# One shifted copy of VectorE's key tiles made by GpSimd in 128x512 pieces, and key products released three slots later

## The chip, the core and the metric

The kernel runs on one core of a Trainium2 chip. The metric is device time in microseconds, from the first to the last instruction and what lies around them; the median of the runs is compared. Engines are called as in the profile: PE (TensorE, matrix products), ACT (ScalarE, exponentials), DVE (VectorE), POOL (GpSimd) and SP (SyncE, whose queue issues most transfers).

## What is computed

A gated mix of an attention block with 32 heads of width 16 and a feed-forward block, for one sequence of 2048 rows of width 512:

```python
qkv = (x @ wqkv).reshape(B, S, 3, H, Dh).transpose(2, 0, 3, 1, 4)
q, k, v = qkv[0], qkv[1], qkv[2]
scores = einsum("bhqd,bhkd->bhqk", q, k) * (Dh ** -0.5)
a = einsum("bhqk,bhkd->bhqd", softmax(scores), v).transpose(0, 2, 1, 3).reshape(B, S, D) @ wo
b = (silu(x @ w_gate) * (x @ w_up)) @ w_down
g = sigmoid((x * gate_w).sum(-1, keepdims=True))
out = g * a + (1 - g) * b
```

The softmax needs 32 x 2048 x 2048 exponentials, far more than anything else that the vector engines do.

## The kernel before

**Units and key tiles.** The 2048 queries are cut into 4 blocks of 512, the 32 heads into 8 groups of 4. A pair of a query block and a head group is a unit; there are 32, and the four units of head group 0 come first. Each unit has 16 key tiles of 128 keys; a key tile is 4 heads x 128 keys x 512 queries, so there are 512 key tiles. A key tile's position in the whole run is a slot.

**Two ways to an exponential.** For most key tiles PE writes scores into a two-bank PSUM tile `s_t`, and ACT makes the exponentials of both banks in one instruction into `e_all` (128x1024). The rest go to DVE. PE writes their scores, head by head, into one-bank tiles `d_t` (function `emit_d`), often beside an `s_t` group in other rows of the array. DVE reads each `d_t` out of PSUM, scales it and adds a constant, and writes it as 16-bit integers: read as bf16, that bit pattern is a first approximation of the exponential (`first`, one instruction of 128x512 for each head, four into one tile `y` of 128x2048). The approximation is then refined in one of two ways. With `groups[n] == 4` DVE makes three copies of `y`, each shifted by another constant (`copy`, one 128x2048 integer addition each, `SHIFTS`), and PE sums `y` and the three copies against the values: four sums over the key tile. With `groups[n] == 2` DVE makes two masked copies (`bits`) and multiplies (`product`, a 128x2048 product of two tensors): two sums. `quad` chooses the second way unless the planner has found idle room on PE.

**Buffers.** `y` and its copies live in seven homes of 128x2048 (`NS`, `home`, `take_home`, `drop`): six of their own (`c_t` in the profile), and as the seventh a piece of memory that belongs to `wd_t` early and to `kaug` later; so the same operation appears in the profile with `c_t`, `wd_t` or `kaug` in its name. A home is free again when PE has summed the copy, or, for `y`, also when DVE no longer reads it.

**What sets the order.** Every instruction of PE, ACT, DVE and SP is put in a fixed order by hand (`ordered`): each follows the one recorded before it on its engine. A planner in the program keeps an estimated time for each engine (`plan.pe`, `plan.dve`, `plan.act`), and picks what to record next. `fill_dve` picks DVE's next work: evictions of `d_t` (`d_wait`, `pay_d`), other evictions that are owed (`owed`, `pay`), and copies, masks and products (`vops`, `pay_v`). The prices are constants in the program. `v_unit` decides whether another key tile goes to DVE, from how far DVE lags behind ACT in the plan.

**Side work on PE.** Query, key and value products, the feed-forward block and the output projection are chains of pieces with a first slot and a deadline (`Pacer`, `pace.add(pieces, release, deadline, ...)`), put between the score groups. `k_pieces(b, tb)` makes the keys of two head groups for one block of 512 rows (`kp` from `xT` and `wqk`); its result goes through `kst` (the tiles `on` or `bblk`) and is sent by DMA from SP into `kaug`, the key tile with four heads at rows 0, 32, 64 and 96. `k0_pieces(tb)` makes the keys of head group 0 directly (`kp` from `xT` and `mt`, where a padded copy of the weights lies).

**Start of the program.** SP loads the rows and transposes of x (`xT`), then the rest of the value weights (`rb`), then the rest of `wqk`. ACT's queue loads the first columns of the weights. The first two score groups need only those.

In the profile, line 168 is the helper that records every PE product, line 171 the one of ACT, line 180 the one of DVE and SP. POOL has memsets of the start alone (lines 254 to 282, 521, 522).

Of the kernel before, what the change touches and what calls it, by code (L numbers as in the profile page):

```python
# [9 lines left out]
ALU = mybir.AluOpType  # L10
# [69 lines left out]
def kernel(  # L80
# [12 lines left out]
    nc = tc.nc  # L93
# [79 lines left out]
    class Ordered:  # L173
# [4 lines left out]
        def __getattr__(self, name):  # L178
            f = getattr(self.engine, name)
            return lambda *a, **kw: ordered(f(*a, **kw))  # L180

    vec = Ordered(nc.vector)
    queue = Ordered(nc.sync)


# [105 lines left out]


    class Plan:
        pe = dve = act = 0.0
        mode = last = None
        seq = 0
        slot = -1
# [13 lines left out]
    FLIP, UNIT_US = 0.105, 0.217  # L311
    TO_ACT, ACT_FIX, ACT_COL, ACT_IN = 0.485, 0.064, 0.4265, 0.167
    ACT_PE, DVE_PE, PE_DVE, ACT_DVE = 0.055, 0.08, 0.24, 0.06

    def spend(mode, mms, ready=0.0):

# [5 lines left out]
    def later(cost, f, ready=None, key=None):  # L322

        c = plan.chain
        if c is not None:
            c.owed += 1
        ready = plan.pe + PE_DVE if ready is None else ready
        owed.insert(sum(o[0] <= ready for o in owed), (ready, cost, f, c, key))

    def spend_v(cost, ready=0.0, key=None):  # L330

        if key is not None and key == plan.last:
            cost += 0.13
        plan.last = key
        plan.dve = max(plan.dve, ready) + cost
# [115 lines left out]
    def k_pieces(b, tb):  # L451

        def end(t, p):
            vec.tensor_copy(out=kst[b][:, t * QBW:(t + 1) * QBW], in_=p[:, :])
            m_free(p, plan.dve)
            if t == QB - 1:
                for hh in range(8):
                    g, j = 2 * b + hh // 4, hh % 4
                    if g > 0:
                        queue.dma_start(out=kaug[32 * j:32 * j + DH, g, :], in_=kst[b][DH * hh:DH * (hh + 1), :])  # L460

        def lhs(dc):
            if dc == 0 and tb == 0:
                kst[b] = (on_t[1], bblk)[b == 1][:, :, :].rearrange("p b q -> p (b q)")
            return wqk[:, dc, D + P * b:D + P * (b + 1)]
        return columns(DC, "kp", lhs, lambda dc: xT[:, dc, tb * QBW:(tb + 1) * QBW],
                       lambda p: later(0.6, lambda: end(tb, p)))
# [365 lines left out]
        users[i] = [1, 0.0]  # L833
        return i, t

    def home(i=None, t=0.0):

        if i is None:
            i, t = take_home()
        plan.dve = max(plan.dve, t)  # L840
        if i < NS - 1:
            return i, vex.tile([P, NV * QBW], U16, tag=f"h{i}", name="c_t", bufs=1)[:, :]
        return i, (kaug[:, 0, :] if au > QB else wd_t[:, 0:4, :].rearrange("p f d -> p (f d)")).bitcast(U16)

    def emit_d(i, rows=32):
        if not vcur:
            n = v_take()
            waiting[n] = [NV, None, take_home()]
            vcur.update(n=n, left=list(range(NV)), y=None)
            y_live[0] += 1  # L850
        n, left, cur = vcur["n"], vcur["left"], waiting[vcur["n"]]
        left.remove(i)
        d_t = m_tile("d_t")
        score(d_t[:, :], 4 * n + i, rows)
        if not left:
            vcur.clear()

        def first():
            if cur[1] is None:
                cur[1] = home(*cur[2])  # L860
            h, y = cur[1]
            vec.tensor_scalar(out=y[:, i * QBW:(i + 1) * QBW], in0=d_t[:, :], scalar1=EXP_A, scalar2=EXP_B[groups[n]],
                              op0=ALU.mult, op1=ALU.add)
            m_free(d_t, plan.dve)
            cur[0] -= 1
            if cur[0]:
                return
            plan.last = ("y", n)
            if groups[n] == 2:
                vops.extend([(0.6, lambda: bits(n, 0, y), ("y", n), n, True), (0.6, lambda: bits(n, 1, y), None, n, True),  # L870
                             (MUL_US, lambda: product(n, h, y), None, n, False)])
            else:
                users[h][0] = 2
                ready(n, 0, h, y)
                for k in range(1, 4):
                    vops.append((0.6, lambda k=k: copy(n, k, h, y), ("y", n) if k == 1 else None, n, True))
        d_wait.append((plan.pe + UNIT_US + PE_DVE, first, n))

    waiting = {}
# [4 lines left out]
        copies[n, k] = (c.bitcast(BF16), h)  # L884
        vready.append((plan.dve + DVE_PE, n, k))

    def copy(n, k, i, y):
        h, c = home()
        vec.tensor_scalar(out=c, in0=y, scalar1=SHIFTS[k - 1], scalar2=None, op0=ALU.add)
        ready(n, k, h, c)  # L890
        if k == 3:
            drop(i, plan.dve + 0.05)
            y_live[0] -= 1

# [16 lines left out]
    def c_ready():  # L911
        return min(c_free) if not vops or vops[0][4] else 0.0
# [5 lines left out]

    def pay_v():
        cost, f, key, _, _ = vops.pop(0)  # L920
        spend_v(cost, 0.0, key)
        f()

    def fill_dve():

        while plan.dve <= plan.pe + 0.2:
            now = plan.dve
            due = [k for k, o in enumerate(owed) if o[0] <= now + 0.05]
            free = [k for k in due if owed[k][4] is None or owed[k][4] != plan.last]
            fit = bool(vops) and vops[0][3] // KT <= closed + AHEAD and c_ready() <= now  # L930
            if fit and vops[0][3] // KT < au and vops[0][2] != plan.last:
                pay_v()
            elif d_wait and d_wait[0][2] // KT < au and d_wait[0][0] <= now + 0.05:
                pay_d()
            elif free:
                pay(free[0])
            elif d_wait and d_wait[0][0] <= now + 0.05:
                pay_d()
            elif fit and vops[0][2] != plan.last:
                pay_v()  # L940
            elif due:
                pay(due[0])
            elif fit:
                pay_v()
            elif d_wait or owed or vops and vops[0][3] // KT <= closed + AHEAD:
                t = min([w[0] for w in d_wait] + [o[0] for o in owed[:1]]
                        + [c_ready()] * bool(vops and vops[0][3] // KT <= closed + AHEAD))
                if t > plan.pe:
                    break
                plan.dve = max(plan.dve, t)  # L950
                plan.last = None
            else:
                break
# [330 lines left out]
    for qb in range(QB):  # L1284
        for b in range(NB):
            d = UNIT.index((qb, max(2 * b, 1))) * KT
            after = []
            if qb == 0:
                ks = []
                for tb in range(QB):  # L1290
                    prev = [pace.add(k_pieces(b, tb), 0, d - 40 + tb, prev)]
                    ks += prev

                def bnd(b=b):
                    later(2.46, lambda: k_bound(b))
                after = prev = [pace.add([(0.2, bnd, False)], 0, d - 34, ks)]

            if b == 0:
                rel = UNIT.index((qb - 1, 2)) * KT + 1 if qb else 0
            elif b == 1:  # L1300
                rel = UNIT.index((qb - 1, 6)) * KT + 1 if qb else 0
            else:
                rel = UNIT.index((qb, 2 * b - 2)) * KT + 1 if (qb, b) != (0, 2) else UNIT.index((0, 2)) * KT + 1
            q = pace.add(q_pieces(qb, b), rel, d - QLEAD, after)
            need.setdefault(d - 12, []).append(q)
            for g in {max(2 * b, 1), 2 * b + 1}:
                q_of[UNIT.index((qb, g))] = q
# [182 lines left out]
    def next_pv():  # L1490
        flush_act()
        while not pv_list(None):
            if d_wait:
                pay_d()
            elif vops and c_ready() < 1e9:
                pay_v()
            elif owed:
                pay()
            else:
                lone_d()  # L1500
        emit_pv(pv_list(None)[0])
# [105 lines left out]
                continue  # L1607
        emit_group(w, ride, rel)
    flush_act()
    while closed < UNITS or vops or vcur:  # L1610
        fill_dve()
        while owed and owed[0][0] <= plan.pe:
            pay()
        if plan.slot < SLOTS + 1:
            begin(plan.slot + 1)
            pace.credit = max(pace.credit, 2.0)
        if vcur:
            lone_d()
            continue
        c = side(2.0)  # L1620
        if not pv_list(plan.pe) and c is not None:
            put_piece(c)
            continue
        if closed == UNITS - 1 and pv_left(closed) <= 2 and not a_ps[2:]:
            tail_ready()
            tail(3)
        next_pv()
# [72 lines left out]
```

## Time and profile before

| | us |
|---|---|
| three runs | 773.22, 774.35, 776.6 |
| median | 774.35 |
| profiled execution, time | 773.97 |
| profiled execution, span from first to last instruction | 772.3 |
| PE busy | 743.8 (96%) |
| DVE busy | 737.9 (96%) |
| ACT busy | 751.0 (97%) |
| POOL busy | 10.6 (1%) |
| granted clock, mean | 0.996 |

The span is shorter than the time by 1.7 us, which lie around the first and the last instruction. A busy time is the union of an engine's instructions; consecutive instructions of DVE and ACT overlap a little, so the mean duration of one is longer than the step from one start to the next. A row of a group gives the instructions' line, engine, operation and tiles, how many there are, then their busy time in microseconds and the mean of one in nanoseconds, then the idle time in front of them and what ended it. A row of a wait gives who waited for whom, the sum in microseconds, how often, and the longest.

### The profile page before, as it was taken

What the parts mean: (1) busy time and instruction counts of PE and PEld (TensorE: products, weight loads), DVE (VectorE), ACT (ScalarE), POOL (GpSimd) and SP (SyncE); (2) the same over time, 40 slices, a digit from 0 to 9 for tenths busy, and PEclk for the clock granted to TensorE, in tenths of its full rate; (3) what the DMA queues carried; (4) which work ended last, traced back from release to release, by engine and by line L of the source; (5) the groups of instructions that cost most, each with busy time, mean ns of one, the idle gap of its engine ahead of it and who ended that gap; (6) DMA issues with size and microseconds to landing.
All of it is one profiled execution on the core that took longest, in us unless ns stands there. A gap on an engine that the chain in (4) does not pass through costs nothing.

```text
span 772.3 us, 24100 instructions
## 1 busy us (share of the span) xinstructions
PE 743.8 (96%) x10072; PEld 245.0 (32%) x10073; DVE 737.9 (96%) x1234; ACT 751.0 (97%) x843; POOL 10.6 (1%) x25
## 2 busy tenths in 40 slices
PE   7999999999999999999999999999999999999997
PEld 2323333333333333233223333333333323333332
DVE  5799999999999999999999999999999999989993
ACT  3999999999999999999999999999999999999996
POOL 5000000000000000000000000000000000000000
PEclk9999999999999999999999999999999999999999
DMA  8002312234120013311100130212000232100001
GB/s 191 1 2 49 63 21 51 58 105 96 36 61 13 17 26 77 72 33 40 39 19 23 45 81 16 66 35 55 18 13 26 60 80 56 31 19 5 22 29 36
DMA packets 91029, 34.53 MB, mean 45 GB/s; under 512 B 75488, under 2 KB 90472, under 8 KB 90920
## 3 DMA queue, kind: packets, MB, share of 16 engines
q1 hardware_dynamic: 89192, 32.66, 17.6%
q8 instruction: 79, 1.29, 0.7%
q10 hardware_dynamic: 1728, 0.33, 0.2%
q14 instruction: 30, 0.25, 0.1%
HBM read 21.55 MB, written 2.35 MB: 31 GB/s over the span
## 4 chain that ended last, share of the span: by engine, by line
ACT 36%; DVE 29%; PE 23%; issue 8%; DMA 2%; SPq 2%; DVEq 0%; ACTq 0%
ACT e_all L171 35%; DVE c_t L180 19%; PE s_t L168 8%; PE o_ps L168 7%; DVE kaug L180 3%; PE gu L168 3%; DVE mt L180 2%; DVE gs L180 2%; SPq L180 2%; PE kp L168 2%; PE ops L168 1%; DVE osb L180 1%; ACT th L171 1%; PE vp L168 1%; DMA wqk<-in_A_wqkv_dram 1%
## 5 line engine op out<-in xcount | busy, mean ns | idle before, releaser
L171 ACT ACTIVATE e_all<-s_t 128x1024 bf16<-128x1024 f32 x774 | 723.3, 1049 | 7.8 <-PE s_t L168 6.1
L180 DVE TENSOR_SCALAR c_t<-d_t 128x512 uint16<-128x512 f32 x432 | 286.7, 684 | 2.1 <-PE d_t L168 1.4
L168 PE MATMUL s_t<-qx,kaug 32*128 32x512 bf16 (+1 forms) x1228 | 238.6, 384 | 10.1 <-ACT e_all L171 9.1
L168 PE MATMUL o_ps<-e_all,vaug 128*32 128x512 bf16 (+3 forms) x2028 | 170.3, 333 | 0.2
L168 PEld LDWEIGHTS <-kaug 32*128 32x128 bf16 (+1 forms) x2048 | 80.8, 91 | 276.2 <-issue 269.6
L180 DVE TENSOR_SCALAR c_t<-c_t 128x2048 uint16<-128x2048 uint16 x234 | 157.7, 685 | 0.8 <-PE o_ps L168 0.4
L168 PE MATMUL d_t<-qx,kaug 32*128 32x512 bf16 x404 | 154.5, 384 | 0.0
L168 PEld LDWEIGHTS <-vaug 128*32 128x32 bf16 x4076 | 100.9, 95 | 133.8 <-issue 99.5
L168 PE MATMUL o_ps<-c_t,vaug 128*32 128x512 bf16 (+3 forms) x1740 | 137.8, 340 | 2.0 <-DVE osb L180 1.1
L168 PE MATMUL gu<-xT,wg 128*32 128x512 bf16 x896 | 72.8, 383 | 0.0
L168 PE MATMUL gu<-xT,wu 128*32 128x512 bf16 x896 | 70.4, 383 | 0.4 <-DVE c_t L180 0.2
L168 PE MATMUL ops<-wd_t,mt 128*32 128x512 bf16 x672 | 56.4, 382 | 0.0
L180 DVE TENSOR_TENSOR c_t<-c_t 128x2048 bf16<-128x2048 bf16 x35 | 42.6, 1217 | 0.0
L180 DVE SCALAR_TENSOR_TENSOR mt<-gs,gu 128x512 bf16<-128x512 bf16 x56 | 38.2, 683 | 3.2 <-PE gu L168 0.9
L168 PE MATMUL s_t<-q,kaug 32*128 32x512 bf16 (+1 forms) x184 | 35.7, 384 | 3.4 <-ACT e_all L171 3.1
L180 DVE SCALAR_TENSOR_TENSOR gs<-th,gu 128x512 bf16<-128x512 bf16 x56 | 38.1, 679 | 0.0
L180 DVE TENSOR_SCALAR kaug<-d_t 128x512 uint16<-128x512 f32 x56 | 37.4, 682 | 0.3 <-PE d_t L168 0.2
L171 ACT ACTIVATE th<-gu 128x512 bf16<-128x512 f32 x56 | 35.0, 624 | 0.0
L168 PEld LDWEIGHTS <-mt 128*32 128x32 bf16 (+1 forms) x1037 | 24.4, 96 | 26.6 <-issue 20.3
L180 DVE TENSOR_SCALAR kaug<-c_t 128x2048 uint16<-128x2048 uint16 x48 | 32.9, 685 | 0.0
L168 PEld LDWEIGHTS <-wu 128*32 128x32 bf16 x896 | 19.2, 95 | 26.2 <-issue 19.7
L168 PE MATMUL d_t<-q,kaug 32*128 32x512 bf16 x72 | 27.3, 384 | 0.0
(142 smaller groups left out, 442.1 us busy)
## 6 DMA issues: line engine op xcount, KB each, us to landing
wg<-in_B_w_gate_dram SPq DMA_DIRECT2D x56, 128.0 KB
wu<-in_B_w_up_dram SPq DMA_DIRECT2D x56, 128.0 KB
on<-osb SPq DMA_DIRECT2D x120, 16.0 KB
rb<-rr SPq DMA_DIRECT2D x15, 128.0 KB
wd_t<-in_B_w_down_dram SPq DMA_DIRECT2D x7, 256.0 KB
qx<-qst SPq DMA_DIRECT2D x96, 16.0 KB
qx<-aq SPq DMA_DIRECT2D x96, 16.0 KB
out_dram<-o_t SPq DMA_DIRECT2D x12, 128.0 KB
```

The costliest lines, as they stand in the source:

```text
L168: return ordered(nc.tensor.matmul(*args, **kw))
L171: ordered(nc.scalar.activation(*args, **kw))
L180: return lambda *a, **kw: ordered(f(*a, **kw))
```

## The change

Three things change.

GpSimd's share: for a key tile with three shifted copies, the third copy is no longer made by DVE in one instruction, but by GpSimd in four pieces of 128x512 (`piece`), if no more than two pieces are still waiting and a home is free (`gives`). The pieces wait in a list, `aside`. One is recorded just before a DVE instruction that reads PSUM (`beside`, called from the new wrapper `Vector`), if the planner thinks GpSimd is idle by then; others are recorded where the planner sees DVE idle. Each piece gets a dependency on the last DVE instruction that did not read PSUM (`last_pass`), so that it starts only behind it. The piece adds the constant and takes the maximum with 0; DVE's copy only adds.

The planner: GpSimd has an estimated time, `plan.pool`, with 0.55 us for a piece (`POOL_US`). A copy, mask or product of DVE is planned no earlier than 0.05 us before GpSimd is idle, and evictions go ahead of it when GpSimd is still busy. Because the planner decides from its estimates what is recorded next, the order of instructions changes on every engine.

The key chains: the release of `k_pieces` moves from slot 0 to slot 3.

```diff
+    class Vector(Ordered):
+
+        def __getattr__(self, name):
+            f = getattr(self.engine, name)
+
+            def g(*a, **kw):
+                read = [v for k, v in kw.items() if k in ("in_", "in0", "in1")] + list(a[1:])
+                psum = any(getattr(getattr(v, "tensor", None), "_space", None) == bass.MemoryType.PSUM for v in read)
+                if psum:
+                    beside()
+                ins = ordered(f(*a, **kw))
+                if not psum:
+                    last_pass[:] = [ins]
+                return ins
+            return g
...
-    vec = Ordered(nc.vector)
+    vec = Vector(nc.vector)
+    gps = Ordered(nc.gpsimd)
...
+    POOL_US = 0.55
...
+    def beside():
+
+        t = plan.dve - 0.6
+        if aside and plan.pool <= t + 0.05 and aside[0](t, True):
+            go(t)
+
+    def go(t):
+        ins = aside.pop(0)(t, False)
+        for i in last_pass:
+            sync(ins, i)
+        plan.pool = max(plan.pool, t + 0.1) + POOL_US
...
-                users[h][0] = 2
+                gives = len(aside) <= 2 and min(c_free) < 1e9
+                users[h][0] = 3 if gives else 2
                 ready(n, 0, h, y)
-                for k in range(1, 4):
-                    vops.append((0.6, lambda k=k: copy(n, k, h, y), ("y", n) if k == 1 else None, n, True))
+                for k in range(1, 3 if gives else 4):
+                    vops.append((0.6, lambda k=k: copy(n, k, h, y, k == (2 if gives else 3)), ("y", n) if k == 1 else None, n, True))
+                if gives:
+                    aside.extend(lambda t, ask, i=i, st=st: piece(n, h, y, st, i, t, ask) for st in [{0: take_home()}] for i in range(4))
...
+    def piece(n, i, y, st, k, t, ask):
+
+        if ask:
+            return st[0][1] <= t
+        if 1 not in st:
+            st[1] = home(*st[0], wait=False)
+        h, c = st[1]
+        cols = slice(k * QBW, (k + 1) * QBW)
+        ins = gps.tensor_scalar(out=c[:, cols], in0=y[:, cols], scalar1=SHIFTS[2], scalar2=0.0, op0=ALU.add, op1=ALU.max)
+        if k == 3:
+            t = max(plan.pool, t + 0.1) + POOL_US
+            copies[n, 3] = (c.bitcast(BF16), h)
+            vready.append((t + DVE_PE, n, 3))
+            drop(i, t + 0.05)
+        return ins
...
     def pay_v():
         cost, f, key, _, _ = vops.pop(0)
-        spend_v(cost, 0.0, key)
+        spend_v(cost, plan.pool - 0.05, key)
         f()
...
             fit = bool(vops) and vops[0][3] // KT <= closed + AHEAD and c_ready() <= now
+            if fit and plan.pool > now + 0.1 and (free or d_wait and d_wait[0][0] <= now + 0.05):
+                fit = False
...
+            elif aside and plan.pool <= now and aside[0](now, True):
+                go(now)
...
-                    prev = [pace.add(k_pieces(b, tb), 0, d - 40 + tb, prev)]
+                    prev = [pace.add(k_pieces(b, tb), 3, d - 40 + tb, prev)]
```

Two loops near the end also empty `aside`. In the instruction orders of the two kernels, 774 exponentials of ACT become 768, 64 key tiles get their third copy from GpSimd (256 pieces), and the 512 key tiles split into 384 for ACT and 128 for DVE, where they were 387 and 125.

More of the change, by code (lines that the diff above doesn't have):

```diff
@@ L180, in __getattr__ @@
             return lambda *a, **kw: ordered(f(*a, **kw))
-    vec = Ordered(nc.vector)
+    class Vector(Ordered):
[11 more added lines that the diff above has]
+            return g
+    last_pass = []
+    aside = []
+    vec = Vector(nc.vector)
+    gps = Ordered(nc.gpsimd)
     queue = Ordered(nc.sync)
@@ L293 @@
     class Plan:
-        pe = dve = act = 0.0
+        pe = dve = act = pool = 0.0
         mode = last = None
@@ L834, in take_home, with home @@
         return i, t
-    def home(i=None, t=0.0):
+    def home(i=None, t=0.0, wait=True):
         if i is None:
             i, t = take_home()
-        plan.dve = max(plan.dve, t)
+        if wait:
+            plan.dve = max(plan.dve, t)
         if i < NS - 1:
@@ L885, in ready, with copy @@
         vready.append((plan.dve + DVE_PE, n, k))
-    def copy(n, k, i, y):
+    def piece(n, i, y, st, k, t, ask):
[12 more added lines that the diff above has]
+        return ins
+    def copy(n, k, i, y, last):
         h, c = home()
@@ L890, in copy @@
         ready(n, k, h, c)
-        if k == 3:
+        if last:
             drop(i, plan.dve + 0.05)
@@ L1498, in next_pv @@
                 pay()
+            elif aside:
+                go(max(plan.dve, plan.pool))
             else:
@@ L1609 @@
     flush_act()
-    while closed < UNITS or vops or vcur:
+    while closed < UNITS or vops or vcur or aside:
         fill_dve()
```

## The prediction

> **What bounds the kernel now.** I read the busy time by stage first, to see which engine has room and where.
>
> ```profile
> 12.50:22.40 9.90, 6.86 (x46) 1.24 (x49) 4.45 (x7) 4.10 (x5) 0.00 (x0) 0.66 0.47 140
> 22.40:700.00 677.60, 659.83 (x9063) 216.44 (x9067) 667.14 (x1102) 675.75 (x759) 0.00 (x0) 1.00 0.18 43
> 700.00:764.00 64.00, 63.31 (x855) 21.04 (x850) 56.38 (x90) 63.81 (x70) 0.00 (x0) 1.00 0.06 17
> ```
>
> Columns: stretch, length, busy microseconds of PE, PEld, DVE, ACT and POOL, granted clock, DMA share, GB/s. From 22.4 to 764 ACT is busy 739.6 of 741.6 us, PE 723.1, DVE 723.5, POOL not at all. ACT sets the pace there, the two others are full to 97%, so a gain needs less work on all three. In the 9.9 us before, ACT is busy 4.1 and the clock averages 0.66: a hole. The table of waits between 22.4 and 764 agrees:
>
> ```profile
> PE s_t L168 <- ACT e_all L171: 13.6, 36, 0.6
> ACT e_all L171 <- PE s_t L168: 0.7, 2, 0.5
> PE o_ps L168 <- DVE c_t L180: 0.8, 3, 0.4
> ```
>
> PE waits for ACT to free a score tile; ACT hardly waits, and DVE's products are nearly never late. Then the timeline of the hole (start, us, what, idle before):
>
> ```profile
> 12.89 0.39 PE L168 MATMUL kp<-xT,wqk 128*32 128x512 bf16 x2
> 13.00 1.02 ACT L171 ACTIVATE e_all<-s_t 128x1024 bf16<-128x1024 f32 x1 [0.50 <-PE s_t L168]
> 16.25 1.04 PE L168 MATMUL kp<-xT,wqk 128*32 128x512 bf16 x6 [2.97 <-DMA wqk<-in_A_wqkv_dram]
> 17.88 1.02 ACT L171 ACTIVATE e_all<-s_t 128x1024 bf16<-128x1024 f32 x1 [3.85 <-PE s_t L168]
> 22.42 12.36 ACT L171 ACTIVATE e_all<-s_t 128x1024 bf16<-128x1024 f32 x13 [0.49 <-PE s_t L168]
> ```
>
> Key products that need wqk stand on PE ahead of the second score group and wait 2.97 us for the load. In finer stretches the clock is 0.50 from 16.0 to 22.4, so the eight-product groups take 1.04 us each, against 0.61 later. ACT's fifth exponential starts at 22.42.
>
> **Part 1: key products released three slots later.** In the changed order PE runs two score groups, then 16 products of the first head group's remaining keys (kp from xT and mt), and the wqk products come only behind the sixth score group. The moved products need no new work. What do the products now in front wait for? The last transposed loads of xT. DMA traffic dips to 50 GB/s at 12.5 to 13.0 and then runs at about 370 until 16.5, and 140 GB/s x 9.9 us = 1.39 MB is what rb and wqk hold (3 x 448 KB): the transposes were in by about 13. wqk is in by 17.0; the sixth group falls at 13.0 + 5 x 0.93 = 17.7. ACT's fifth exponential can start at 13.0 + 4 x 0.93 = 16.7 (0.93 = 723.3 us / 774), 5.7 us earlier. Bounds: 3.0 (only the load's wait goes, the half clock stays) and 5.8 (all ACT idle in that stretch). I take 5.7: PE then has 32 key products (8 x 0.22) and five score groups in some 4 us, and no long idle. DVE's first work on kp, at 20.38 before, starts behind its memsets, which end at 15.92, so it moves 4.5 us forward.
> Queues: the key rows (4 DMAs kaug<-on, 60.33 before) now stand on SP behind wo_t and wo_l (0.59 + 3.72 us of issue); their first reader is a product at 107.92, so some 40 us of other units cover it. If that cover went, PE would wait up to 4.3 us.
>
> **Part 2: one of three copies goes to GpSimd.** Counts come from the instruction orders of both kernels. Of 512 key tiles 125 were exponentiated on DVE, now 128: 66 by three shifted copies (78 before) and 62 by two masks and a product (47 before). 64 third copies become 256 GpSimd pieces of 128x512.
>
> ```profile
> L180 DVE TENSOR_SCALAR c_t<-d_t 128x512 uint16<-128x512 f32 x432 | 286.7, 684 | 2.1 <-PE d_t L168 1.4
> L180 DVE TENSOR_SCALAR c_t<-c_t 128x2048 uint16<-128x2048 uint16 x234 | 157.7, 685 | 0.8 <-PE o_ps L168 0.4
> L180 DVE TENSOR_TENSOR c_t<-c_t 128x2048 bf16<-128x2048 bf16 x35 | 42.6, 1217 | 0.0
> 327.49 0.69 DVE L180 TENSOR_SCALAR c_t<-c_t 128x2048 uint16<-128x2048 uint16 x1
> 328.08 1.28 DVE L180 TENSOR_SCALAR c_t<-d_t 128x512 uint16<-128x512 f32 x2
> 329.28 0.68 DVE L180 TENSOR_SCALAR c_t<-c_t 128x2048 uint16<-128x2048 uint16 x1
> ```
>
> Passes and PSUM reads last 0.68 but start 0.60 apart, which is their price. DVE: 70 passes fewer (328 to 258), -42.0; 12 reads more, +7.2; 15 products more at 1.14 (0.08 overlap), +17.1: -17.7 us. ACT: 774 to 768 exponentials, -6 x 0.93 = -5.6. PE: 6 score groups fewer and 21 sums over a key tile fewer (384 + 264 + 124 against 387 + 312 + 94), 27 x 0.22 (two sums start at 300.82 and 301.04) = -5.9. So ACT and PE fall together by 5.6, and DVE has 17.7 - 5.6 = 12.1 us to spare. That spare is what the pieces may cost DVE.
>
> **What a piece costs.** No row of before has it. The nearest, all POOL:
>
> ```profile
> L263 POOL MEMSET ident<- 128x128 bf16 x1 | 0.2, 206 | 0.3 <-POOLq L1684 0.3
> L521 POOL MEMSET q<- 128x1024 bf16 x1 | 1.0, 958 | 0.0
> L264 POOL TENSOR_SCALAR_AFFINE_SELECT ident<-ident 128x128 bf16<-128x128 bf16 x1 | 0.3, 295 | 0.0
> L270 POOL MEMSET vaug<- 128x512 bf16 x1 | 2.3, 2282 | 0.0
> ```
>
> The dense memsets give 0.10 + 0.835 per 1000 elements, 0.53 for 512. The select, which also reads, is 0.10 + 1.52 per 1000: 0.88 for 512. The strided memset of 512 took 2.28. Bounds 0.53 and 2.28; I take 0.55, by the dense rows, since a piece is dense and does only an add and a max. That is the weakest choice here.
> The Trainium skill (GPSIMD Engine Reference, Elementwise — side-by-side cycle accounting) gives 1.03 cycles an element for bodies of up to two operations and about 1.8 for longer ones; as an estimate from that page a piece is 0.44 us at 1.2 GHz and its dispatch, which is the dense row again, and the longer body is the select's rate.
>
> **What a piece does to DVE.** Each piece waits for DVE's last SBUF pass, so it runs under the PSUM reads that follow. The casts of tp at about 7 us took 686 ns with POOL at work, as alone: reads of PSUM are not slowed. The question is the next SBUF pass. Bounds: not disturbed, 0; or held until the piece ends. Under the second a window of m reads and n pieces overruns by 0.2 + n x P - 0.6 m: 0.08 since the pass ends after the next read has begun, about 0.07 for a semaphore (0.05 in the rows), the rest for the second wait that many pieces carry. In the new order 127 windows hold pieces; in 71 n equals m (30 with 1, 29 with 2, 8 with 3, 4 with 4), the rest have more reads. At P = 0.55: 30 x 0.15 + 29 x 0.10 + 8 x 0.05 = 7.8 us. With a delay of 0.1 or 0.3 in place of 0.2 it is 1.5 or 14.9. I take the held case. 7.8 is under the spare 12.1, but the spare does not lie where the overruns lie: products c_t come later by tenths, and a score group behind them on PE's queue is late. I let a quarter of 7.8, 2.0 us, reach ACT; bounds 0 and 7.8.
> The Trainium skill (SBUF — State Buffer, Who interferes with whom) states that a VectorE instruction using both its ports and a GpSimd one lock each other out for a whole instruction; by that the held case is the right one, and no row of before can show it.
> Behind a late piece on POOL wait only later pieces; for its last one waits a sum on PE (o_ps from c_t), and DVE for the tile it reads.
>
> **Sum.** 773.97 (the profiled execution: span 772.3 and 1.7 around it) - 5.7 - 5.6 + 2.0 = 764.7. The median of the runs, 774.35, is 0.4 above that execution, so I say 765.
>
> **Rivals.**
> *A, the forecast*, 765, own range 762.7 (no overrun) to 770.5 (7.8 reaches ACT in full). Chance 0.58.
> *B, part of the gain is eaten.* Pieces of 0.62 to 0.67, or later starts: at 0.62 the windows give 6.6 + 7.0 + 2.1 + 1.1 = 16.8, at 0.67 23.2. Beyond the spare DVE sets the end: 762.7 + (16.8 - 12.1) = 767.4, or 773.8. For it: select reads and is slower; against: it does more per element. Chance 0.17, half of it within 0.5%.
> *C, slower: DVE becomes the bound through held passes.* It decides from P = 0.67, where the overrun of 23.2 has used up the spare and nearly all of the 11.3 us gained. At 0.70 the overrun is 27.0: 777.6. At the select's 0.88 it is 50.0 in the equal windows and 7.5 in the others, 57.5: 808. For it: the only POOL row with an input runs at that rate, 71 windows leave no room, and DVE is 98% full. Against: the dense rows. Chance 0.20.
> *D, the first part does not do what it says*: the products put in front wait for transposes, the hole stays. 774.0 - 5.6 + 2.0 = 770.4. Against: the dip at 12.5. Chance 0.05.
>
> **How the numbers follow.** 0.5% (3.9 us) is what this measurement can tell from no change: below 770.5 is faster, above 778.2 slower. Faster: A 0.57, half of B 0.08, half of D 0.02, 0.67. Slower: C less what falls below 778, 0.19. Same: 0.14. The range: from 761, under A's end, up to 783, a piece of about 0.73; above that and below lie about 0.2, nearly all C.
>
> **What would show it.** Part 1: the wait for wqk gone from PE, the clock 1.0 from 12.5 to 22.4, the fifth exponential near 16.7. Part 2: 256 POOL pieces of about 0.55, 258 passes, 768 exponentials, ACT still busy over 99% between 22 and 750. Overrun: DVE idle or long passes right behind pieces, some 8 us in all. I am wrong if pieces last over 0.65, if passes stretch by more than 0.1 on the mean, or if PE's waits for c_t grow past a few us.

## The result, and the profile after

The changed kernel takes 1011.81 us (median of 4 runs, 1010.27 to 1016.0) against 774.27 before (4 runs, 773.22 to 776.6): ratio 1.3071, 95% interval 1.3022 to 1.312. The forecast was 765, the range 761 to 783. The change costs some 237 us.

The page of the changed kernel, busy time, granted clock and the shares of the chain that ended last:

```profile
PE 849.3 (84%) x10025; PEld 251.5 (25%) x10025; DVE 755.3 (75%) x1191; ACT 762.2 (76%) x837; POOL 522.9 (52%) x281
PEclk9979999799998889779889888998899898988989
POOL 39%; PE 25%; DVE 16%; ACT 8%; issue 6%; SPq 0%; DMA 0%; POOLq 0%; DVEq 0%; ACTq 0%
```

The first row gives each engine's busy time, share of the span and number of instructions; the second the granted clock in 40 equal slices, in tenths; the third the chain. No engine is full any more: ACT, 97% before, is at 76%. POOL works 523 us and holds 39% of the chain, where it had no share before. The stages, with the columns of before:

```profile
12.50:22.40 9.90, 9.08 (x108) 2.53 (x105) 7.91 (x14) 9.41 (x11) 0.00 (x0) 1.00 0.66 206
22.40:1000.00 977.60, 826.49 (x9810) 242.79 (x9810) 737.35 (x1140) 745.51 (x816) 511.86 (x256) 0.90 0.13 30
```

The first stretch is the good half of the change: the hole is gone, the clock stays at 1.00, ACT is busy 9.4 of 9.9 us (4.1 before). ACT's timeline there:

```profile
12.75 1.94 ACT L171 ACTIVATE e_all<-s_t 128x1024 bf16<-128x1024 f32 x2 [0.50 <-PE s_t L168]
14.93 8.36 ACT L171 ACTIVATE e_all<-s_t 128x1024 bf16<-128x1024 f32 x9 [0.24 <-PE s_t L168]
```

The fifth exponential is the third of the second row and starts near 14.93 + 2 x 0.93 = 16.8 (22.42 before). In the second stretch the clock is 0.90, and PE, DVE and ACT have all become idle for some 150 to 240 us. The groups and the waits say for whom they wait:

```profile
L180 POOL TENSOR_SCALAR c_t<-c_t 128x512 uint16<-128x512 uint16 x184 | 370.1, 2035 | 323.7 <-DVE c_t L192 180.4
L192 DVE TENSOR_SCALAR c_t<-c_t 128x2048 uint16<-128x2048 uint16 x183 | 135.8, 747 | 4.9 <-PE o_ps L168 2.9
```

```profile
ACT e_all L171 <- PE d_t L168: 169.8, 108, 5.8
DVE c_t L192 <- PE d_t L168: 169.6, 106, 7.0
PE o_ps L168 <- POOL c_t L180: 122.8, 91, 2.5
```

A piece lasts 2.04 us, not 0.55, so a copy of four takes 8.1 us. PE's sums over GpSimd's copies stand in its fixed queue where the plan expected the copy, and PE stops there 101 times, 134 us in all (122.8 and two smaller rows for the homes in `kaug` and `wd_t`). The scores for ACT and DVE stand behind, so both wait for PE. One such place:

```profile
323.66 8.43 POOL L180 TENSOR_SCALAR c_t<-c_t 128x512 uint16<-128x512 uint16 x4 [17.45 <-DVE c_t L192]
...
325.93 0.77 DVE L192 TENSOR_SCALAR kaug<-c_t 128x2048 uint16<-128x2048 uint16 x1
...
327.52 0.38 PE L168 MATMUL o_ps<-c_t,vaug 128*32 128x512 bf16 x1 [0.86 <-POOL c_t L180]
330.26 0.58 PE L168 MATMUL o_ps<-c_t,vaug 128*32 128x512 bf16 x1 [2.37 <-POOL c_t L180]
332.15 0.59 PE L168 MATMUL o_ps<-c_t,vaug 128*32 128x512 bf16 x1 [1.30 <-POOL c_t L180]
```

Four pieces, and PE takes up one head's sum after each. A pass is one of DVE's 128x2048 instructions from SBUF to SBUF. DVE's pass at 325.93 runs while the pieces follow each other without a gap and takes 0.77 us in place of 0.68: it is not held until a piece ends. The longest pass of this trace takes 1.14.

### The profile page after: what moved, and what is told of

Read it like the earlier page. It is cut to its first block, busy times and chain, and to the rows that moved or that the text cites. A ratio compares the mean times of both kernels' runs of the same rounds, so it can differ in the third digit from the quotient of the medians.

```text
span 1008.5 us, 24263 instructions
## 1 busy us (share of the span) xinstructions
PE 849.3 (84%) x10025; PEld 251.5 (25%) x10025; DVE 755.3 (75%) x1191; ACT 762.2 (76%) x837; POOL 522.9 (52%) x281
## 4 chain that ended last, share of the span: by engine, by line
POOL 39%; PE 25%; DVE 16%; ACT 8%; issue 6%; SPq 0%; DMA 0%; POOLq 0%; DVEq 0%; ACTq 0%
POOL c_t L180 33%; DVE c_t L192 11%; PE s_t L168 9%; PE o_ps L168 8%; ACT e_all L171 7%; POOL kaug L180 4%; PE gu L168 4%; PE ops L168 1%; DVE kaug L192 1%; PE dps L168 1%; POOL wd_t L180 1%; PE qp L168 1%; DVE mt L192 1%; DVE gs L192 1%; DVE qst L192 1%
## 5 line engine op out<-in xcount | busy, mean ns | idle before, releaser
L180 POOL TENSOR_SCALAR c_t<-c_t 128x512 uint16<-128x512 uint16 x184 | 370.1, 2035 | 323.7 <-DVE c_t L192 180.4
L192 DVE TENSOR_SCALAR c_t<-d_t 128x512 uint16<-128x512 f32 x428 | 287.6, 684 | 171.4 <-PE d_t L168 169.6
L168 PE MATMUL o_ps<-c_t,vaug 128*32 128x512 bf16 (+3 forms) x1692 | 181.1, 365 | 124.3 <-POOL c_t L180 122.8
L168 PE MATMUL s_t<-qx,kaug 32*128 32x512 bf16 (+1 forms) x1208 | 254.0, 417 | 7.8 <-ACT e_all L171 6.7
L168 PE MATMUL o_ps<-e_all,vaug 128*32 128x512 bf16 (+3 forms) x2056 | 190.3, 359 | 0.5 <-ACT e_all L171 0.4
L168 PE MATMUL d_t<-qx,kaug 32*128 32x512 bf16 x424 | 173.4, 419 | 0.5 <-DVE qx L192 0.3
L180 POOL TENSOR_SCALAR c_t<-kaug 128x512 uint16<-128x512 uint16 x40 | 78.9, 1993 | 117.3 <-DVE c_t L192 101.8
L192 DVE TENSOR_SCALAR c_t<-c_t 128x2048 uint16<-128x2048 uint16 x183 | 135.8, 747 | 4.9 <-PE o_ps L168 2.9
L180 POOL TENSOR_SCALAR kaug<-c_t 128x512 uint16<-128x512 uint16 x24 | 48.2, 2030 | 21.8 <-DVE c_t L192 21.8
L192 DVE TENSOR_TENSOR c_t<-c_t 128x2048 bf16<-128x2048 bf16 x47 | 58.0, 1234 | 0.0
L168 PE MATMUL o_ps<-kaug,vaug 128*32 128x512 bf16 (+3 forms) x228 | 26.5, 374 | 8.4 <-POOL kaug L180 8.4
```

What stands on the lines that cost most here:

```text
L168: return ordered(nc.tensor.matmul(*args, **kw))
L192: ins = ordered(f(*a, **kw))
```

## The experiments

Two theories stood against each other. Price: a piece costs 2 us by itself, the plan puts the sums for 0.55, and PE waits. Contention: GpSimd and VectorE keep each other out of SBUF, so pieces and passes stretch each other.

**The release alone** (e1_release): the kernel before with this line only.

```diff
-                    prev = [pace.add(k_pieces(b, tb), 0, d - 40 + tb, prev)]
+                    prev = [pace.add(k_pieces(b, tb), 3, d - 40 + tb, prev)]
```

> The kernel before with one edit: the key chains are released at slot 3, nothing goes to GpSimd. If the hole at the start was worth what the working says, 5.7 us go: 768.6. Rival: the time is lost again later, because VectorE or a later deadline sets the pace, and the time stays within 1 us of 774.3.

Measured: 768.94 us, ratio 0.9933 (0.992 to 0.9945): 5.1 us gained by 774.0 measured beside it. The fifth exponential starts at 16.9 here (15.04 + 2 x 0.93) and the clock is 1.00 from 12.5 to 22.4. The first part does what it was read to do, a little less than 5.7.

**What kinds of GpSimd instruction cost** (e2_forms): added to the kernel before, on dead columns of `wqk`; nothing waits for them. `two` is the piece's operation (an addition and a maximum), `single` the addition alone, `pair` the addition of a second tensor as 32-bit integers; `n` is 512.

```diff
+        st = [wqk[:, i, D:2 * D].bitcast(U16) for i in range(4)]
...
+        run(16, two, st[0], st[1])
+        run(16, lambda to, x: gps.tensor_copy(out=to, in_=x), st[0], st[1])
+        run(16, single, st[0], st[1])
+        run(16, two, st[0].bitcast(BF16), st[1].bitcast(BF16))
+        run(16, pair, st[0].bitcast(I32), st[1].bitcast(I32))
+        run(16, two, st[0][:, 0:n // 2], st[1][:, 0:n // 2])
+        run(16, two, st[0].bitcast(F32), st[1].bitcast(F32))
+        run(16, lambda to, x: gps.memset(to, 1.0), st[0], None)
```

> The kernel before, with eight kinds of GpSimd instruction, 16 of each, on dead columns of wqk that nobody reads, from about 180 us on. Theory: a piece costs about 1.9 us by itself, because of the operation and its 16-bit operands, so the first kind shows a minimum of 1.9 us here too, and half of its elements about 1.0. Rival: it costs about 0.55 us alone and is stretched by VectorE in the changed kernel; then the shortest of the 16 is near 0.55. Which kinds are cheap is open: single addition, plain copy, bf16 or f32 operands, 256 integer pairs; the memset should be 0.53.

The rows of these tiles by stretch; the three numbers are shortest, median and longest in ns:

```profile
L180 POOL TENSOR_SCALAR wqk<-wqk x16: 1917/2062/2720, 181.7 to 215.3; 128x512 uint16<-128x512 uint16 x16
L180 POOL COPY wqk<-wqk x16: 610/613/1537, 217.3 to 229.9; 128x512 uint16<-128x512 uint16 x16
L180 POOL TENSOR_SCALAR wqk<-wqk x17: 1487/1805/2401, 231.0 to 262.0; 128x512 uint16<-128x512 uint16 x16, 128x512 bf16<-128x512 bf16 x1
L180 POOL TENSOR_SCALAR wqk<-wqk x16: 1917/1920/3339, 262.0 to 294.8; 128x512 bf16<-128x512 bf16 x16
L180 POOL TENSOR_TENSOR wqk<-wqk x16: 723/761/1120, 298.2 to 312.3; 128x256 int32<-128x256 int32 x16
L180 POOL TENSOR_SCALAR wqk<-wqk x16: 1064/1094/1488, 313.5 to 332.3; 128x256 uint16<-128x256 uint16 x16
L180 POOL TENSOR_SCALAR wqk<-wqk x17: 1064/1192/1905, 332.3 to 353.7; 128x256 f32<-128x256 f32 x16, 128x256 uint16<-128x256 uint16 x1
L180 POOL MEMSET wqk<- x16: 524/524/951, 355.2 to 366.5; 128x512 uint16 x16
```

The shortest of 16 is 1.917, so the price is the operation's own. From 256 to 512 elements it rises by 0.853 us, 3.33 ns an element, about 0.21 fixed. The third row is the single addition (and one bf16 instruction that falls into the same stretch): shortest 1.487, so leaving out the maximum saves 0.43. bf16 operands cost as much as uint16, and 256 elements of f32 as much as 256 of uint16 (the shortest of the 16 is 1.064 too), so this operation's price goes by the element and not by the byte. The plain copy is 0.61; the memset is 0.524, as the memset rows of before gave it (0.53). The same bytes as 256 integers of 32 bits, added to a second tensor, take 0.72. This kernel, run once, took 789.81 us, 15.8 more than the 774.0 beside it, with VectorE busy 753.3 us in place of 737.9.

**Contention without waiting** (e3_loose): the 256 pieces, beside the orders of before on PE, ACT, DVE and SP.

```diff
+    def loose():
+
+        to, x = [wqk[:, i, D:2 * D].bitcast(U16) for i in range(2)]
+        for _ in range(256):
+            gps.tensor_scalar(out=to, in0=x, scalar1=SHIFTS[2], scalar2=0.0, op0=ALU.add, op1=ALU.max)
```

> The kernel before, with 256 pieces as in the changed kernel on dead columns of wqk, which wait for nobody and on which nobody waits; PE, ACT and VectorE run the orders of before. Theory (the loss comes from products that wait for late copies): some 490 us of pieces beside the others, VectorE's SBUF passes longer by 0.06 us as in the changed kernel (about 250 passes in that time, 15 us of VectorE at most), time between 774 and 790. Rival (the loss comes from the two engines holding each other's SBUF accesses): each pass waits for the rest of a piece, about 1 us on the mean, some 200 us more: 900 to 1000.

Measured: 805.74 us, ratio 1.0404 (1.0375 to 1.0432). The passes of before (first block) and the pieces and passes of this run (second), shortest, median, longest, then two passes in order of time:

```profile
L180 DVE TENSOR_SCALAR c_t<-c_t x234: 675/685/695, 38.3 to 756.1; 128x2048 uint16<-128x2048 uint16 x117
```

```profile
L180 POOL TENSOR_SCALAR wqk<-wqk x256: 1917/2131/3338, 178.9 to 753.4; 128x512 uint16<-128x512 uint16 x128
L180 DVE TENSOR_SCALAR c_t<-c_t x234: 674/689/1148, 37.9 to 789.4; 128x2048 uint16<-128x2048 uint16 x117
...
401.65 1.10 DVE L180 TENSOR_SCALAR c_t<-c_t 128x2048 uint16<-128x2048 uint16 x1
402.68 1.28 DVE L180 TENSOR_SCALAR kaug<-d_t 128x512 uint16<-128x512 f32 x2
403.88 0.88 DVE L180 TENSOR_SCALAR c_t<-c_t 128x2048 uint16<-128x2048 uint16 x1
```

From 200 to 700 us POOL is busy 481.7 of 500 us, so nearly every pass has a piece beside it. Between 180 and 750 us the median of the largest group is still 0.691, its mean 0.800, and the longest pass is 1.148: at most 0.46 us more than 0.685, though a piece lasts 1.9 or longer. Over the whole trace the 328 passes take 28 us more than at 0.685 each, and the 47 products 3 us more than before. Together that is nearly the 31.7 us that the kernel lost against 774.0. So contention is real, more than the theory's 15, and far under the rival's 200. In the changed kernel, where the mean of the largest group of passes is 0.747, all 258 together lose about 16 us.

**The right price in the planner** (e5_nohold, e4_price).

```diff
-    POOL_US = 0.55
+    POOL_US = 2.0
...
-        spend_v(cost, plan.pool - 0.05, key)
+        spend_v(cost, 0.0, key)
...
-            if fit and plan.pool > now + 0.1 and (free or d_wait and d_wait[0][0] <= now + 0.05):
-                fit = False
```

> The changed kernel with the planner's price of a piece at 2.0 us in place of 0.55, and without the planner's rule that VectorE's passes wait for GpSimd to be idle. Theory (late copies against the plan are the loss): the plan now expects a copy some 8 us after its first piece, PE's waits for GpSimd fall from 134 us to under 20, and the time comes to 765 to 790. Rival (GpSimd's use as such is the loss): the time stays above 900.

> The changed kernel with the planner's price of a piece at 2.0 us and its rule that passes wait for GpSimd kept. Against e5_nohold (791.8) it tells what the rule costs when the price is right. Theory (passes need no hold): the plan now idles VectorE beside pieces, more key tiles go to ACT, and it is slower than e5_nohold, 800 to 850. Rival (the rule saves what contention cost): faster than 791.8.

e4_price has the first of the three edits alone. One run each: 791.84 without the rule, 827.84 with it. Both are new orders: 54 and 65 copies come from GpSimd in place of 64, and ACT makes 772 and 804 exponentials in place of 768. In e5_nohold no product of PE waits for GpSimd, against 134 us, with pieces still at 2.0 us. So 184 of the 237 us go away with the price alone in the plan, and 220 when the rule goes as well; the second time is 2 us above the range that was given. With the rule the kernel is 36 us slower at that price, as expected, though its order differs in more than the rule. e5_nohold still stands 23 us above the release alone. What these are made of was not taken apart; pieces of 2 us did not pay in either of these orders.

**The price itself** (e6_pair): the orders of PE, ACT, DVE and SP are the changed kernel's, and only the piece's operation differs. It adds a constant tile `shifts`, made at the start, and leaves out the maximum with 0.

```diff
-        ins = gps.tensor_scalar(out=c[:, cols], in0=y[:, cols], scalar1=SHIFTS[2], scalar2=0.0, op0=ALU.add, op1=ALU.max)
+        ins = gps.tensor_tensor(out=c[:, cols].bitcast(mybir.dt.int32), in0=y[:, cols].bitcast(mybir.dt.int32), in1=shifts[:, 0:1].bitcast(mybir.dt.int32).broadcast_to([P, QBW // 2]), op=ALU.add)
```

> The changed kernel, instruction order kept on PE, ACT, VectorE and SyncE; each piece is done on the same bytes as 256 integers of 32 bits, a TENSOR_TENSOR addition of a constant that holds the shift in both halves. That kind took 0.72 to 0.76 us where it ran loose, 1.9 the other. Theory (the loss is the piece's price against the planned 0.55): nearly all of the 237 us goes, time 764 to 780, PE's waits for GpSimd from 134 us to under 15. Rival (GpSimd beside VectorE costs as such, whatever its price): two inputs read more, the time stays above 850.

Measured: 768.36 us, ratio 0.9923 (0.9905 to 0.9941). Two rows of its trace:

```profile
L180 POOL TENSOR_TENSOR c_t<-c_t,shifts 128x256 int32<-128x256 int32 x184 | 108.9, 611 | 403.8 <-DVE c_t L192 233.6 <-PE d_t L168 92.7 <-PE gu L168 20.6
L192 DVE TENSOR_SCALAR c_t<-c_t 128x2048 uint16<-128x2048 uint16 x183 | 125.7, 692 | 1.0 <-PE o_ps L168 0.3
```

Pieces of 0.61 us in the same order, and 243 us are gone. No product of PE waits for GpSimd any more; one weight load does, for 0.5 us. Passes are at 0.692 against 0.685, some 2 us in all, so hardly any lateness or contention is left. The loss was the price of the operation in an order made for 0.55 us. Contention of the dearer operation went with it; e3_loose puts that at 31.7 us where nobody waits.

The same run shows what the change is worth without that loss. It is 0.6 us below the release alone (768.94), and the two intervals overlap: in this order GpSimd's share is not shown to gain anything.

**The price doubled** (e9_double): the piece's line of e6_pair twice.

```diff
+        gps.tensor_tensor(out=c[:, cols].bitcast(mybir.dt.int32), in0=y[:, cols].bitcast(mybir.dt.int32), in1=shifts[:, 0:1].bitcast(mybir.dt.int32).broadcast_to([P, QBW // 2]), op=ALU.add)
         ins = gps.tensor_tensor(out=c[:, cols].bitcast(mybir.dt.int32), in0=y[:, cols].bitcast(mybir.dt.int32), in1=shifts[:, 0:1].bitcast(mybir.dt.int32).broadcast_to([P, QBW // 2]), op=ALU.add)
```

> As e6_pair, with every piece done twice in place (the second writes the same values again), so a piece costs about 1.22 us; the orders of PE, ACT, VectorE and SyncE are those of the changed kernel. Between e6_pair (0.61 us, 768.4) and the changed kernel (2.02 us, 1011.8) a straight line gives 768.4 + 243.4 x 0.61 / 1.41 = 874. Theory (each late copy stops PE once the slack is used up): on or below the line, 820 to 880, PE's waits for GpSimd near half of 134 us. Rival (slow clock after PE's pauses makes most of the loss, which sets in only with long pauses): far below the line, under 800, with the granted clock above 0.98.

```profile
L180 POOL TENSOR_TENSOR c_t<-c_t,shifts 128x256 int32<-128x256 int32 x368 | 259.4, 721 | 309.2 <-DVE c_t L192 264.2 <-DVE kaug L192 8.8 <-DVE kb L192 6.4
```

```profile
PE o_ps L168 <- POOL c_t L180: 46.7, 46, 2.4
```

Measured: 848.53 us, ratio 1.0958 (1.0892 to 1.1024), within the theory's 820 to 880. Two instructions took 1.44, not 1.22. PE's products wait 49.6 us for GpSimd (46.7 and two smaller rows), less than the half of 134 that the theory gave; the clock is above 0.98, as the rival had it, but the time is not under 800. From 0.61 to 1.44 the kernel loses 80 us on 212 us of POOL work (256 x 0.83), 0.38 us for each of GpSimd's; from 1.44 to 2.04, where the operation changes too, it loses 163 on 154, 1.06 for each. That the first step is cheaper because the order leaves some room between a copy and its sum is likely, but not shown.

What the loss is made of shows in PE's busy time, first in e6_pair, then in e9_double:

```profile
PE 741.2 (97%) x10024; PEld 243.4 (32%) x10025; DVE 726.3 (95%) x1191; ACT 747.2 (97%) x837; POOL 161.9 (21%) x282
PE 770.8 (91%) x10024; PEld 243.9 (29%) x10025; DVE 751.8 (89%) x1191; ACT 754.9 (89%) x837; POOL 372.2 (44%) x538
```

The spans are 766.5 and 847.1 us, and 1008.5 in the changed kernel, where PE is busy 849.3. So PE is idle 25.3, 76.3 and 159.2 us: 51 and 134 more than in e6_pair, which is what its products wait for GpSimd (49.6 and 134.1). The rest, 30 and 108 us, is PE needing longer for the same products. In the changed kernel, then, 134 of the 242 us are pauses and 108 slower products. Two things make them slower. The granted clock is 0.999, 0.984 and 0.902; as an estimate, 741 us at 0.902 would be 821, 80 of the 108. And sums that wait for a piece each no longer run side by side: in the changed kernel four together take 0.39 us at 321.82, and one alone 0.38 to 0.59 at 327.52, 330.26 and 332.15. How the 108 divide between the two was not measured. Contention does not make the steeper part: all passes together are some 14 us longer than 0.685 each in e9_double and 16 in the changed kernel.

**The cheap piece in other orders** (e7_pair80, e8_pair80nh, e10_pair70): e6_pair with the planner's price at 0.8, the same without the rule that holds passes, and with 0.7. The line of e7_pair80:

```diff
-    POOL_US = 0.55
+    POOL_US = 0.8
```

> As e6_pair, with the planner's price of a piece at 0.8 us in place of 0.55, so a new order (770 exponentials on ACT in place of 768). Theory: the copies come when the plan says, PE waits for GpSimd under 5 us, and the time is that of the release alone, 768.9, less up to 3.7 for four exponentials fewer: 765 to 770. Rival (what is left is contention of the SBUF accesses, not lateness): no better than e6_pair.

> As e7_pair80, without the planner's rule that VectorE's passes wait until GpSimd is idle. Theory (a pass beside a piece is stretched by about 0.1 us, not held for it): no slower than e7_pair80, 763 to 770. Rival (the accesses exclude each other for a whole instruction, so the rule earns its place): slower than e7_pair80 by 10 us or more.

> As e7_pair80, with the planner's price at 0.7 us in place of 0.8, nearer to the 0.61 that the pieces take. If the price is what matters, 764 to 767, no slower than e7_pair80 (765.9) by more than 1 us. If what the order happens to be matters as much, anything from 763 to 770.

e7_pair80: 765.92 us, ratio 0.9891 (0.9873 to 0.9909), the best here, and its interval lies below that of the release alone (0.992 to 0.9945). e8_pair80nh: 767.85, ratio 0.9916 (0.9894 to 0.9937): 1.9 us above e7_pair80, neither what the theory said nor the rival's 10. Its order differs in more than the rule (768 exponentials for 770), so at this price the rule is worth 2 us or less. e10_pair70: 772.65, ratio 0.9972 (0.9959 to 0.9984), outside both expectations: a price nearer to the true one gave a worse order. Its waits show where some of it went:

```profile
ACT e_all L171 <- PE s_t L168: 6.0, 7, 3.6
DVE on L192 <- PE kp L168: 3.9, 3, 3.3
PE d_t L168 <- DMA qx<-aq: 2.3, 1, 2.3
```

The longest waits of these rows stand in one place, between 122.9 and 128 us: PE stops 2.31 us at a `d_t` product for a load of queries, and the clock is 0.50 from 125.5 to 131.0 (1.00 before). That is a hole of the kind that the release had closed, products of PE behind a load. Four orders with the cheap piece lie between 765.9 and 772.7 us, with the release alone at 768.9 among them. One of the four is better than it beyond the intervals, by 3.0 us, and one is worse; so the order that the planner happens to make weighs more here than GpSimd's share.

## Why the prediction was wrong

**What bounds the kernel, and part 1: right.** ACT at the pace, PE and DVE full behind it. The hole closed as read: fifth exponential at 16.8 (forecast 16.7), clock 1.00. The release alone brought 5.1 us for 5.7.

**The counts of part 2: right, as far as they go.** 768 exponentials and 256 pieces came as counted, and with cheap pieces the same order gives 768.4. Between 22.4 and 758 us ACT is idle 5.2 us there (735.6 less 730.4) against 2.0 before (22.4 to 764). Of the 9.3 us that the sum gave net, 6.1 were got (774.47 beside it, less 768.36). Of these the release accounts for 5.1. For GpSimd's share the sum gave 3.6 (5.6 less 2.0); against the release alone 0.6 came out, within the noise. ACT is busy 3.6 us less than there (747.2 for 750.8), but idle 2.9 us more.

**"What a piece costs": the step that failed.** The prediction took 0.55 by the dense memset rows, "since a piece is dense and does only an add and a max". The price is 1.92 undisturbed (the shortest in e2_forms) and 2.04 on the mean in the changed kernel. A memset neither reads nor computes; the plain copy, which reads, would indeed be 0.61, but the addition and the maximum cost 3.33 ns an element, as uint16 or bf16. The stated upper bound, the strided memset's 2.28, was the nearest row by number, by luck, since it is another operation; and the range was then cut at a piece of 0.73. The only row with an input and arithmetic, the select, gave 1.52 an element and should have been the low end, not only a ground for the rivals. The Trainium skill (GPSIMD Engine Reference, Elementwise — side-by-side cycle accounting) was read as speaking for 0.55, with 1.03 cycles an element for two operations; at its 1.2 GHz the measured 3.33 ns are 4.0 cycles, so the measurement decides against it for this operation. The 1.8 that the prediction takes from it is there the best case of one unrolled loop, not the rate of all longer bodies.

**"What a piece does to DVE": wrong in size, and as the mechanism.** Passes were taken as held until the piece ends. At 0.61 the window count gives 15.5 us of overrun in the equal windows; the passes of e6_pair are 7 ns longer on the mean in the largest group (692 for 685), some 2 us in all. In e3_loose no pass was held for more than 0.46 us. The rule of the Trainium skill (SBUF — State Buffer, Who interferes with whom), that the second instruction is blocked for the whole of the first, does not describe the passes of these runs.

**What was not priced: a late copy.** The prediction named the sum on PE that waits for the last piece and put no time on it; its 2.0 us stand for late passes of DVE. With pieces of 0.61 that would have held, since no product waited in e6_pair. At the true price it is the bound: PE's fixed queue stops at each copy, 134 us in all, and holds back the scores of both other engines; and PE's products took 108 us longer, which the prediction's sum has no term for either.

**The rivals.** B's number was met by e6_pair (767.4 at 0.62, measured 768.4 at 0.61), but not by its mechanism, so that is luck: in e6_pair the passes overrun by 2 us and not by 17. C was on the right side, with the wrong bound: DVE is 75% busy, not full. Its own count at the measured 2.04 gives 198 us of overrun in the equal windows alone and so 949 us (762.7 + 198 - 12), not far from 1011.8; but the passes' real overrun is 16 us, and DVE's largest wait is 169.6 us for PE's scores. It set the threshold at 0.67 and gave a chance of 0.20 to pieces that cost too much. D is excluded by e1_release. Of the signs named beforehand, pieces over 0.65 and PE's waits for c_t were the two that showed; the mean pass grew by 0.06, under the 0.1 named.

## What to carry to other kernels

The price of an instruction that a trace does not hold is not the price of another instruction of the same engine and size: run sixteen of it on dead memory beside the kernel before planning with it. In an order fixed by hand a wrong price is paid by the engine whose queue holds the consumer and by all work behind it, here up to 1.06 us for each further us of GpSimd's work; the busy share of the engine that is late (52%) shows nothing of it. An integer addition to 16-bit values can be done on pairs, if no carry can cross; that took the price from 1.92 to 0.61 and the loss away, though the gain that is left is 3 us at best and depends on the order.

## What the runs showed of the hardware that was not expected

GpSimd, 128x512 of 16 bits: memset 0.524 us, copy 0.61, an addition of a scalar and a maximum 1.92 (uint16 and bf16), 1.06 for half the elements (uint16, and also f32), the addition alone from 1.49 on (all in e2_forms). As 256 pairs with a full second tensor 0.72 (e2_forms), with a second input of one element repeated 0.61 (e6_pair). Beside VectorE both sides stretch: pieces from 1.92 to 2.17 on the mean in e3_loose, passes by up to 0.46 us, more than half of them by less than 0.02; reads of PSUM kept their 0.68. PE: after one pause of 2.31 us the granted clock stood at 0.50 from 125.5 to 131.0 us (e10_pair70).
